# A fused mLSTM and two-layer MoE kernel: the state decay moves from a DRAM round trip and GpSimd to ScalarE and the broadcast in PSUM, and ScalarE's first queue is reordered

## The chip, the cores and the metric

The kernel runs on one core of a Trainium2 chip. A core has five engines with a queue each, which run in order and meet through semaphores: TensorE (PE; its weight loads are listed as PEld), VectorE (DVE), ScalarE (ACT), GpSimd (POOL) and SyncE (SP), which here issues all the DMAs. The metric is the device time of one execution in microseconds (us), as the median of several runs.

## The reference

Three stages follow each other; what counts is cut out here:

```
for t in range(S):                            # S = 768, batch 2, 8 heads, D = 40
    m_new  = max(f[t] + m, i[t])
    f_stab = exp(f[t] + m - m_new);  i_stab = exp(i[t] - m_new)
    C = f_stab * C + i_stab * outer(v[t], k[t])
    n = f_stab * n + i_stab * k[t]
    y[t] = sigmoid(o[t]) * (C @ q[t]) / max(|n . q[t]|, 1)
x = y as [1536, 320]
x = max(x @ w1, x @ w2, x @ w3) @ w_out       # 320 -> 768 -> 320
x = (h * tanh(softplus(h))) @ w_out2, h = x @ w_in   # 320 -> 2048 -> 320
```

## The kernel before

The recurrence is done in chunks of 128 steps. There are six chunks and two batches, so twelve units, numbered u = 2c + b for chunk c and batch b. For a unit, spread(u) makes PE broadcast the decay factors of all eight heads over the partitions (fp), decay(u) makes DVE scan them into the matrix of decays dt, scores(u) gives the products of keys and queries, decayed(u) multiplies the two, and numer(u) multiplies the result by the values. For chunks after the first, passed(u) makes PE broadcast the products of decays since the chunk's start (cp, 120 partitions: three heads of 40 rows), queries(u) multiplies the queries by them on DVE (cb), and numer(u) adds the part that comes from the state st of the batch. denom, gated, transpose_x and lower_x finish a unit: division, output gate, transposition, and the split of x into a rounded part xh and a rest xl, so that products in a rounded format keep precision. outer(u) gives the new part of the state (sp) and carry(u) adds it: state = state x decay of the whole chunk + masked new part.

The decay of a whole chunk comes from the running product cpr (16 partitions, one for each batch and head, 640 columns). Before the change its last column of each chunk goes to DRAM and is read back broadcast over all partitions (dsd, decs). The rest of cpr goes into the rows of fzr from 64 (rounded by ACT) and from 96 (the rest, by POOL), from which PE makes fp and cp of the later chunks.

Weights arrive as 64-bit words; each block is decoded by one ACT instruction (dec, L279) and three DVE instructions (low and dec, L286, L288, L290), and split into a rounded part (ACT, L301 to L303) and a rest (POOL, L304 to L306). Three buffers (raw) hold undecoded blocks.

The order of the first four units and of the first products is written out by hand in mlstm_moe_kernel (L384 to L541), engine by engine in program order. From PLAN0 on, the steps of the plans (a unit's first half a, its second half b, the products u, the weights w and o) are put into order by a scheduler in the framework; with issue_after, nothing of PLAN0 is put on an engine ahead of the instruction that is named (fence for PE, fdve for DVE, fpool for POOL, fsp for SP; ACT has none before the change). After PLAN1 come the second layer's weights and its products; that part isn't touched.

ACT has one table of functions loaded at a time; Exp and Sigmoid need different ones, and the load stands in ACT's queue as an instruction of its own.

Of the kernel before, what the change touches and what calls it, by code (L numbers as in the profile page):

```python
# [22 lines left out]
BH = B * H  # L23
VD = D + 1
# [13 lines left out]
NU = NC * B  # L38
# [4 lines left out]
def mlstm_moe_kernel(ctx, tc, fi0, fir, qk2, q3, nat, w13, wo1, wi2, wo2, ident, bmask, out):  # L43
    nc = tc.nc
# [2 lines left out]
    wpool = ctx.enter_context(tc.tile_pool(name="wpool", bufs=1))  # L47
    stage = ctx.enter_context(tc.tile_pool(name="stage", bufs=1))
    zpool = ctx.enter_context(tc.tile_pool(name="zpool", bufs=1))
    dram = ctx.enter_context(tc.tile_pool(name="dram", bufs=1, space=bass.MemoryType.DRAM))  # L50
    mmp = ctx.enter_context(tc.tile_pool(name="mmp", bufs=3, space=PSUM))

    zraw = zpool.tile([P, 3, NT], F32, tag="zraw", name="zraw")
# [6 lines left out]
    ac = at.enter_context(tc.tile_pool(name="ac", bufs=1))  # L60
    a2 = at.enter_context(tc.tile_pool(name="a2", bufs=2))
    pat = at.enter_context(tc.tile_pool(name="pat", bufs=1, space=PSUM))

    def bank(tag, name):
        if tag == "mm":
            return mmp.tile([P, 512], F32, tag=tag, name=name)
        return pat.tile([P, 512], F32, tag=tag, bufs=3 if tag == "sm" else 1, name=name)
# [4 lines left out]
    idt = ac.tile([P, P + 2 * BH + 1], F32, tag="idt", name="idt")  # L72
    idr = ac.tile([P, 4 * L], F32, tag="idr", name="idr")
    bmt = ac.tile([120, H], F32, tag="bmt", name="bmt")
    decs = ac.tile([P, BH, NC - 1], F32, tag="decs", name="decs")
    kps = [ac.tile([P, 9, D], F32, tag=f"kp{i}", name=f"kp{i}") for i in range(2)]
    vps = [ac.tile([P, 9, VD], F32, tag=f"vp{i}", name=f"vp{i}") for i in range(2)]
    qall = ac.tile([P, 2, 2, 4, L], F32, tag="qs", name="qall")
# [4 lines left out]
    fzr = ac.tile([P, (NC - 1) * L], F32R, tag="fzr", name="fzr")  # L83
# [21 lines left out]
    NR = NC - 1  # L105
# [6 lines left out]
    mtr = scr[0:BH, 3:5].rearrange("p k f -> p (k f)")[:, 0:LR + 1]  # L112
    cpr = scr[64:64 + BH, 4]
    z1r = scr[64:64 + BH, 5]
    dsd = dram.tile([BH, NR], F32, tag="dsd", name="dsd")

    unit = {u: {} for u in range(NU)}
    warm = zraw[:, 0, 0:256].bitcast(mybir.dt.bfloat16)
# [15 lines left out]
    def spread(u, tags=("sc0", "sc1")):  # L134
        c, b = u // B, u % B
        src = fzs if c == 0 else fzr[:, (c - 1) * L:c * L]
        fps = []
        for j in range(2):
            fp = bank(tags[j], f"fp{u}_{j}")
            for hh in range(4):  # L140
                r = b * H + 4 * j + hh
                nc.tensor.matmul(fp[:, hh * L:(hh + 1) * L], sel[:, r:r + 1].to_broadcast([P, P]), src, start=True, stop=True)  # L142
            fps.append(fp)
        unit[u]["fp"] = fps

    def passed(u, tag="sm"):
        c, b = u // B, u % B
        if c == 0:
            return
        ps = bank(tag, f"cp{u}")[0:120, 0:3 * L].rearrange("p (g t) -> p g t", g=3)  # L150
        for g in range(3):
            r = b * H + 3 * g
            nc.tensor.matmul(ps[:, g], sel40[:, r * D:(r + 3) * D], fzr[:, (c - 1) * L:c * L], start=True, stop=True)
        unit[u]["cp"] = ps

    def scores(u, banks=None):
        qk = qks[u % 2]
# [32 lines left out]
    def dummy(ps, n):  # L190
        for _ in range(n):
            nc.tensor.matmul(ps, warm[:, 0:P], warm, start=True, stop=True)  # L192
# [14 lines left out]

    def denom(u):
        num = unit[u]["it"]
        nq = a2.tile([P, H, 1], F32, tag="nq", name=f"nq{u}")  # L210
        den = a2.tile([P, H, 1], F32, tag="den", name=f"den{u}")
        nc.vector.tensor_scalar(nq, num[:, :, D:VD], -1.0, 1.0, op0=ALU.mult, op1=ALU.max)
        nc.vector.tensor_tensor(den, num[:, :, D:VD], nq, op=ALU.max)
        nc.vector.reciprocal(den, den)
        sg = unit[u]["sg"]
        nc.gpsimd.tensor_tensor(sg, sg, den.to_broadcast([P, H, D]), op=ALU.mult)
# [8 lines left out]
    def transpose_x(u, xp=None, fill=0):  # L225
        xh, xl = xs[u // 4]
        col = u % 4 * L
        xn = unit[u]["xn"]
        xp = bank("sm", f"xp{u}") if xp is None else xp
        dummy(xp, fill)  # L230
        xp = xp[:, 0:3 * L].rearrange("p (j t) -> p j t", j=3)
        for j in range(3):
            nc.tensor.transpose(xp[:, j], xn[:, j * P:(j + 1) * P], idt[:, 0:P])
        nc.scalar.activation(xh[:, :, col:col + L], xp, AF.Copy)  # L234
        unit[u]["xp"] = xp

    def lower_x(u):
        xh, xl = xs[u // 4]
# [17 lines left out]
    def carry(u):  # L256
        c, b = u // B, u % B
        sp = unit[u]["sp"]
        if c == 0:
            return nc.vector.tensor_tensor(st[b], sp[:, 0:H], bmt[:, 0:H].unsqueeze(2).to_broadcast([120, H, VD]), op=ALU.mult)  # L260
        nw = a2.tile([120, H, VD], F32, tag="nw", bufs=1, name=f"nw{u}")
        nc.vector.tensor_tensor(nw, sp[:, 0:H], bmt[:, 0:H].unsqueeze(2).to_broadcast([120, H, VD]), op=ALU.mult)
        nc.gpsimd.tensor_tensor(st[b], st[b], decs[0:120, b * H:(b + 1) * H, c - 1:c].to_broadcast([120, H, VD]), op=ALU.mult)
        nc.gpsimd.tensor_tensor(st[b], st[b], nw, op=ALU.add)

    raws = {}

# [116 lines left out]
    with tc.manual_schedule(engines={ET.PE, ET.DVE, ET.SP, ET.Activation, ET.Pool}):  # L384
# [46 lines left out]
        nc.scalar.activation(gT0, gp[:, 0:BH], AF.Copy)  # L431
        nc.vector.tensor_copy(zs[:, :, 0:1], fs[:, :, 0:1])
        nc.vector.memset(fs[:, :, 0:1], 0.0)
        scores(0)
        spread(1, ("sm", "sm"))
        scores(1, [bank("mm", "sc1_0"), bank("mm", "sc1_1")])
# [6 lines left out]
        gateo(0)  # L443
        decay(1)
        load_qk(2)
        nc.gpsimd.tensor_tensor(ir, ir, mr, op=ALU.subtract)
        values(1)
        keys(1)
        decayed(1, 0)
# [10 lines left out]
        denom(0)  # L460
        carry(0)
        nc.vector.tensor_tensor_scan(cpr, fr, z1r, 0.0, op0=ALU.mult, op1=ALU.add)
        nc.scalar.activation(ir, ir, AF.Exp)
        nc.sync.dma_start(dsd, cpr.rearrange("p (c t) -> p c t", c=NR)[:, :, L - 1])
        load_nat(3)
        nc.sync.dma_start(decs, dsd.rearrange("h c -> (h c)").partition_broadcast(P))
        fetch(w13[1], "w13_1")
        decay(2)
        gated(0)
        nc.scalar.activation(fzr[64:64 + BH], cpr, AF.Copy)  # L470
        it1 = bank("sm", "it1")
        dummy(it1, 3)
        numer(1, it1)
# [1 line left out]
        for c in range(NR):  # L475
            nc.tensor.transpose(gq[:, c * BH:(c + 1) * BH], ir[:, c * L:(c + 1) * L], idt[0:BH, 0:BH])
        scores(2, [bank("sm", "sc2_0"), bank("mm", "sc2_1")])
        nc.gpsimd.tensor_tensor(fzr[96:96 + BH], cpr, fzr[64:64 + BH].bitcast(F32), op=ALU.subtract)
        keys(2)
        nc.scalar.activation(gTr, gq[:, 0:NR * BH], AF.Copy)  # L480
        denom(1)
# [1 line left out]
        decayed(2, 0)  # L483
        decayed(2, 1)
        spread(3)
        xp0 = bank("mm", "xp0")
        dummy(xp0, 3)
        transpose_x(0, xp0)
        passed(2, "mm")
        values(2)  # L490
        scaled(w13[0], "w13_0")
        mg = merge("w13_0")
# [39 lines left out]
        fsp = fetch(w13[3], "w13_3")  # L532
        fence = outer(3, bank("sm", "sp3"))
        lower_x(2)
        transpose_x(3, bank("sm", "xp3"), 6)
        fetch(w13[2], "w13_2")
        fdve = lower_x(3)
        fpool = load_w13(1)
# [33 lines left out]
        for step in plan.split():  # L572
            act[step[0]](*[int(n) for n in step[1:].split(".")])

    with tc.issue_after(fence.ins), tc.issue_after(fdve.ins), tc.issue_after(fpool.ins), tc.issue_after(fsp.ins):
        follow(PLAN0)
    follow(PLAN1)
    at.close()
# [183 lines left out]
```

## Time and profile before

| | |
|---|---|
| median of 3 runs | 420.75 us (420.63 to 421.41) |
| profiled execution | 419.39 us |
| its span, first to last instruction | 417.6 us |
| PE busy | 401.2 us (96%) |
| DVE busy | 222.7 us (53%) |
| ACT busy | 164.7 us (39%) |
| POOL busy | 163.5 us (39%) |
| mean granted PE clock | 0.975 of full speed |

The busy times are those of one profiled execution. The share of the span is an average over stages of different kinds, so what an engine's work is worth is to be read stage by stage. The granted clock has two levels, 1.00 (2.4 GHz) and 0.50 (1.2 GHz); a value between is a mean over a stretch.

### The profile page before, as it was taken

How to read it: one execution, taken by the hardware profiler on the slowest of the kernel's cores; microseconds unless marked ns; L12 is line 12 of the kernel's file. 1: busy time of each engine (PE TensorE's matmuls, PEld its weight loads, DVE VectorE, ACT ScalarE, POOL GpSimd, SP SyncE). 2: the span in 40 equal slices, each digit the busy share in tenths (PEclk: the TensorE clock that was granted, in tenths of full speed). 3: DMA queues.
4: the chain of work that ended last, by engine and by line, in shares of the span. 5: the costliest groups of instructions: out<-in, count | busy, mean ns of one | idle time of the engine just before them, and what ended most of it. 6: DMA issues, size and time to landing. Idle time of an engine off the chain costs nothing.

```text
span 417.6 us, 6152 instructions
## 1 busy us (share of the span) xinstructions
PE 401.2 (96%) x2385; PEld 351.7 (84%) x2385; DVE 222.7 (53%) x334; ACT 164.7 (39%) x349; POOL 163.5 (39%) x163
## 2 busy tenths in 40 slices
PE   8979599997999999999999999999999999999996
PEld 4858488885879888888888888999988889999996
DVE  7957599989944644523852568993221112222221
ACT  3525354634222122127351657565332233434331
POOL 6645499798443322336772165654000000001000
PEclk9969798998999999999999999999999999999999
DMA  7669464571740300000430042500010000100000
GB/s 209 165 63 294 153 198 168 175 239 65 240 159 2 97 2 0 2 0 2 126 126 2 1 151 102 173 17 0 2 63 2 0 2 0 65 0 2 33 0 33
DMA packets 10650, 32.66 MB, mean 78 GB/s; under 512 B 1645, under 2 KB 4525, under 8 KB 10621
## 3 DMA queue, kind: packets, MB, share of 16 engines
q1 hardware_dynamic: 10621, 32.27, 25.4%
q8 instruction: 19, 0.31, 0.3%
q14 instruction: 10, 0.08, 0.1%
HBM read 30.30 MB, written 1.97 MB: 77 GB/s over the span
## 4 chain that ended last, share of the span: by engine, by line
PE 75%; DVE 11%; POOL 7%; issue 4%; DMA 2%; ACT 1%; POOLq 0%; DVEq 0%; ACTq 0%
PE h L333 21%; PE mm L333 16%; PE o L657 7%; PE o L655 7%; PE o L656 7%; PE it L205 2%; DVE dt L127 2%; DMA raw_w<-in_w_dram 2%; PE mz L365 2%; PE mz L363 2%; PE mz L364 2%; PE wps L192 1%; POOL w L304 1%; PE fp L142 1%; PE sc L161 1%
## 5 line engine op out<-in xcount | busy, mean ns | idle before, releaser
L639 DVE TENSOR_TENSOR gl<-g,gh 128x512 fp32r<-128x512 f32 (+1 forms) x64 | 38.3, 599 | 97.2 <-ACT g L638 97.2
L333 PE MATMUL mm<-xh,w 128*128 128x512 f32 x270 | 76.8, 413 | 3.5 <-ACT xh L234 3.1
L333 PE MATMUL h<-zh,wi 128*128 128x512 f32 (+1 forms) x320 | 66.9, 338 | 0.0
L333 PEld LDWEIGHTS mm<-xh,w 128*128 128x128 f32 x270 | 51.8, 198 | 15.1 <-ACT xh L234 3.2
L637 ACT ACTIVATE gh<-h 128x512 fp32r<-128x512 f32 (+1 forms) x64 | 31.4, 491 | 83.7 <-PE h L333 77.7
L657 PE MATMUL o<-wo,gl 128*128 128x320 f32 x192 | 59.4, 309 | 0.0
L656 PE MATMUL o<-wo,gh 128*128 128x320 f32 x192 | 59.4, 309 | 0.0
L655 PE MATMUL o<-wo,gh 128*128 128x320 f32 x192 | 59.2, 309 | 0.0
L333 PEld LDWEIGHTS h<-zh,wi 128*128 128x128 f32 x320 | 51.4, 189 | 4.8
L608 POOL TENSOR_TENSOR zl<-zraw,zh 128x512 fp32r<-128x512 f32 (+1 forms) x12 | 14.2, 1194 | 91.9 <-ACT zh L607 91.8
L333 PE MATMUL mm<-xl,w 128*128 128x512 f32 x162 | 48.2, 404 | 0.0
L333 PE MATMUL h<-zl,wi 128*128 128x512 f32 (+1 forms) x192 | 44.5, 338 | 0.0
L352 POOL TENSOR_TENSOR hl<-zraw,hh 128x512 fp32r<-128x512 f32 x18 | 25.6, 1422 | 44.2 <-ACT hh L351 44.1
L349 DVE TENSOR_TENSOR zraw<-zraw,mm 128x512 f32<-128x512 f32 x36 | 24.5, 681 | 31.0 <-PE mm L333 30.8
L655 PEld LDWEIGHTS o<-wo,gh 128*128 128x128 f32 x192 | 36.1, 188 | 1.3
L656 PEld LDWEIGHTS o<-wo,gh 128*128 128x128 f32 x192 | 36.1, 188 | 1.2
L333 PEld LDWEIGHTS mm<-xl,w 128*128 128x128 f32 x162 | 31.3, 196 | 6.7
L657 PEld LDWEIGHTS o<-wo,gl 128*128 128x128 f32 x192 | 36.1, 188 | 0.0
L333 PEld LDWEIGHTS h<-zl,wi 128*128 128x128 f32 x192 | 31.8, 188 | 4.1
L638 ACT ACTIVATE g<-h 128x512 f32<-128x512 f32 (+1 forms) x64 | 31.2, 487 | 0.0
L127 DVE TENSOR_TENSOR_SCAN dt<-fp,idr 128x512 f32<-128x512 f32 x24 | 28.3, 1208 | 2.4 <-PE fp L142 2.3
L205 PE MATMUL it<-vp,dt 128*128 128x41 f32 x192 | 25.2, 273 | 0.0
(137 smaller groups left out, 638.4 us busy)
## 6 DMA issues: line engine op xcount, KB each, us to landing
raw_wo<-in_wo_dram SPq DMA_DIRECT2D x11, 640.0 KB
na<-in_nat_dram SPq DMA_DIRECT2D x12, 484.0 KB
raw_w<-in_w_dram SPq DMA_DIRECT2D x9, 640.0 KB
raw_wi<-in_wi_dram SPq DMA_DIRECT2D x8, 640.0 KB
qall<-in_qk_dram SPq DMA_DIRECT2D x24, 160.0 KB
out_dram<-ob SPq DMA_DIRECT2D x12, 160.0 KB
q<-in_q_dram SPq DMA_DIRECT2D x10, 180.0 KB
idt<-in_ident_dram SPq DMA_DIRECT2D x1, 80.5 KB
```

The costliest lines, as they stand in the source:

```text
L127: nc.vector.tensor_tensor_scan(dtf[:, j * 512:(j + 1) * 512], unit[u]["fp"][j], idr, 0.0, op0=ALU.mult, op1=ALU.add)
L205: nc.tensor.matmul(it[:, h], t["dt"][:, h], vt[:, h], start=(c == 0), stop=(c == 0 or h == h1 - 1))
L333: nc.tensor.matmul(ps, a, r, start=(k == 0), stop=(k == 7))
L349: nc.vector.tensor_tensor(top, top, pss[i], op=ALU.max)
L352: nc.gpsimd.tensor_tensor(ls, top, h.bitcast(F32), op=ALU.subtract)
L608: nc.gpsimd.tensor_tensor(zl[:, j], zv[:, j], zh[:, j].bitcast(F32), op=ALU.subtract)
L637: mark[blk, m] = nc.scalar.activation(gh, ps, AF.Mish)
L638: nc.scalar.activation(g, ps, AF.Mish)
L639: low[blk, m] = nc.vector.tensor_tensor(gl, g, gh.bitcast(F32), op=ALU.subtract)
L655: nc.tensor.matmul(po, a, whi, start=(m == 0), stop=False)
L656: nc.tensor.matmul(po, a, wlo, start=False, stop=False)
L657: nc.tensor.matmul(po, l, whi, start=False, stop=(m == KF2 - 1))
```

## The change

The chunk's decay is no longer sent through DRAM. passed(u) copies the last column of cp of each of the three groups out of PSUM into a small tile dc (one ACT instruction). carry(u) scales the state with it in place, three ACT instructions (one for each group of heads, with a scale for each partition), and adds the masked new part with three DVE instructions in place of one; POOL's two instructions of carry and the tile nw go. In the first part that is ordered by hand: the exponential of the later chunks' input gates (ir) and the subtraction ahead of it are moved up, before ACT's first table change; the rounding of cpr into fzr and the subtraction behind it are moved up to where the write to DRAM stood; cp of unit 2 is put ahead of the first transposition, with one dummy product less; and PLAN0 is held back on ACT as well, behind xh of unit 3. denom saves a tile.

```
@@ passed
         unit[u]["cp"] = ps
+        if u < NU - B:
+            dc = a2.tile([120, 3, 1], F32, tag="dc", name=f"dc{u}")
+            nc.scalar.activation(dc, ps[:, :, L - 1:L], AF.Copy)
+            unit[u]["dc"] = dc
@@ denom
-        nq = a2.tile([P, H, 1], F32, tag="nq", name=f"nq{u}")
...
-        nc.vector.tensor_tensor(den, num[:, :, D:VD], nq, op=ALU.max)
+        nc.vector.tensor_scalar(den, num[:, :, D:VD], -1.0, 1.0, op0=ALU.mult, op1=ALU.max)
+        nc.vector.tensor_tensor(den, den, num[:, :, D:VD], op=ALU.max)
@@ carry
-        nw = a2.tile([120, H, VD], F32, tag="nw", bufs=1, name=f"nw{u}")
-        nc.vector.tensor_tensor(nw, sp[:, 0:H], bmt[:, 0:H].unsqueeze(2).to_broadcast([120, H, VD]), op=ALU.mult)
-        nc.gpsimd.tensor_tensor(st[b], st[b], decs[0:120, b * H:(b + 1) * H, c - 1:c].to_broadcast([120, H, VD]), op=ALU.mult)
-        nc.gpsimd.tensor_tensor(st[b], st[b], nw, op=ALU.add)
+        dc = unit[u]["dc"]
+        for g in range(3):
+            h1 = min(3 * g + 3, H)
+            nc.scalar.activation(st[b][:, 3 * g:h1], st[b][:, 3 * g:h1], AF.Copy, scale=dc[:, g])
+        for j in range(3):
+            nc.vector.scalar_tensor_tensor(st[b][:, j::3], sp[:, j:H:3], bmt[:, j:j + 1], st[b][:, j::3], op0=ALU.mult, op1=ALU.add)
@@ order of the first units
         nc.gpsimd.memset(fzr.bitcast(F32), 0.0)
+        nc.gpsimd.tensor_tensor(ir, ir, mr, op=ALU.subtract)
...
         nc.vector.memset(fs[:, :, 0:1], 0.0)
+        nc.scalar.activation(ir, ir, AF.Exp)
...
         load_qk(2)
-        nc.gpsimd.tensor_tensor(ir, ir, mr, op=ALU.subtract)
...
         nc.vector.tensor_tensor_scan(cpr, fr, z1r, 0.0, op0=ALU.mult, op1=ALU.add)
-        nc.scalar.activation(ir, ir, AF.Exp)
-        nc.sync.dma_start(dsd, cpr.rearrange("p (c t) -> p c t", c=NR)[:, :, L - 1])
+        nc.scalar.activation(fzr[64:64 + BH], cpr, AF.Copy)
+        nc.gpsimd.tensor_tensor(fzr[96:96 + BH], cpr, fzr[64:64 + BH].bitcast(F32), op=ALU.subtract)
         load_nat(3)
-        nc.sync.dma_start(decs, dsd.rearrange("h c -> (h c)").partition_broadcast(P))
         fetch(w13[1], "w13_1")
         decay(2)
         gated(0)
-        nc.scalar.activation(fzr[64:64 + BH], cpr, AF.Copy)
...
-        nc.gpsimd.tensor_tensor(fzr[96:96 + BH], cpr, fzr[64:64 + BH].bitcast(F32), op=ALU.subtract)
...
         spread(3)
+        passed(2, "mm")
         xp0 = bank("mm", "xp0")
-        dummy(xp0, 3)
+        dummy(xp0, 2)
         transpose_x(0, xp0)
-        passed(2, "mm")
...
-        transpose_x(3, bank("sm", "xp3"), 6)
+        fact = transpose_x(3, bank("sm", "xp3"), 6)
...
-    with tc.issue_after(fence.ins), tc.issue_after(fdve.ins), tc.issue_after(fpool.ins), tc.issue_after(fsp.ins):
+    with tc.issue_after(fence.ins), tc.issue_after(fdve.ins), tc.issue_after(fpool.ins), tc.issue_after(fsp.ins), tc.issue_after(fact.ins):
         follow(PLAN0)
```

The order on ACT in the first units, from the first gates to gTr, was this before (scr is the scratch tile that holds ir and cpr, sel the selection tile sel40, sg the gates of units 0 and 1, dl and xn those of the next units):

```order
L437 ACTIVATE fzr<-scr 16x640
L187 ACT_TABLE_LOAD
L187 ACTIVATE sg_229<-na_123 128x320
L131 ACTIVATE dl_234<-dt_231 128x8
L187 ACTIVATE sg_274<-na_130 128x320
L459 ACTIVATE sel_99<-idt 128x680
L463 ACT_TABLE_LOAD
L463 ACTIVATE scr<-scr 16x640
L131 ACTIVATE dl_297<-dt_294 128x8
L222 ACTIVATE xn_299<-xn_299 128x64
L470 ACTIVATE fzr<-scr 16x640
L480 ACTIVATE gTr<-gpr 128x80
```

After the change the same stretch of ACT's queue reads:

```order
L437 ACTIVATE scr<-scr 16x640
L441 ACTIVATE fzr<-scr 16x640
L188 ACT_TABLE_LOAD
L188 ACTIVATE sg_227<-na_119 128x320
L128 ACTIVATE dl_232<-dt_229 128x8
L188 ACTIVATE sg_271<-na_126 128x320
L462 ACTIVATE sel_96<-idt 128x680
L466 ACTIVATE fzr<-scr 16x640
L128 ACTIVATE dl_292<-dt_289 128x8
L222 ACTIVATE xn_294<-xn_294 128x64
L480 ACTIVATE gTr<-gpr 128x80
```

The exponential has gone ahead of the first table load, the second load is gone, and the second rounding into fzr stands ahead of dl and xn instead of behind them.

Further on in ACT's queue, around the last transposition of the first four units (sg_627 and sg_717 are the gates of units 4 and 5, xp_486 and xp_507 the transposed x of units 2 and 3), the order before is:

```order
L279 ACTIVATE dec_w_1_478<-raw_w_1_292 128x640
L187 ACTIVATE sg_627<-na_586 128x320
L234 ACTIVATE xh_107<-xp_486 128x3x128
L222 ACTIVATE xn_496<-xn_496 128x64
L187 ACTIVATE sg_717<-na_676 128x320
L279 ACTIVATE dec_w_2_571<-raw_w_2_518 128x640
L234 ACTIVATE xh_107<-xp_507 128x3x128
L301 ACTIVATE w_1_521<-dec_w_1_478 128x512
```

And after the change (st_98 and st_99 are the states of the two batches, now scaled here):

```order
L281 ACTIVATE dec_w_1_471<-raw_w_1_287 128x640
L235 ACTIVATE xh_103<-xp_479 128x3x128
L222 ACTIVATE xn_489<-xn_489 128x64
L235 ACTIVATE xh_103<-xp_500 128x3x128
L303 ACTIVATE w_1_514<-dec_w_1_471 128x512
L304 ACTIVATE w_1_514<-dec_w_1_471 64x128
L305 ACTIVATE w_1_514<-dec_w_1_471 64x128
L264 ACTIVATE st_98<-st_98,dc_352 120x123 x2
L264 ACTIVATE st_98<-st_98,dc_352 120x82
L264 ACTIVATE st_99<-st_99,dc_408 120x123 x2
L264 ACTIVATE st_99<-st_99,dc_408 120x82
L281 ACTIVATE dec_w_2_568<-raw_w_2_511 128x640
```

Both xh now stand ahead of the two gates and of dec_w_2, and six state scalings have come between w_1 and dec_w_2.

SP's queue, from the third unit's loads on (dsd is the tile in DRAM, na_287 the load of unit 3), is this before:

```order
L94 DMA qall<-in_qk_dram 40x1024 x2
L464 DMA dsd<-scr 80x1x1
L98 DMA na_287<-in_nat_dram 128x968
L102 DMA q_289<-in_q_dram 120x384
L466 DMA decs<-dsd 128x80
L271 DMA raw_w_1_292<-in_w_dram 128x1280
L271 DMA raw_w_3_500<-in_w_dram 128x1280
```

And after the change:

```order
L92 DMA qall<-in_qk_dram 40x1024 x2
L96 DMA na_283<-in_nat_dram 128x968
L100 DMA q_285<-in_q_dram 120x384
L273 DMA raw_w_1_287<-in_w_dram 128x1280
L273 DMA raw_w_3_493<-in_w_dram 128x1280
```

The write to DRAM and the read back are gone from between the loads; the rest keeps its order.

## Rows read from the trace of the kernel before

**Rows 1.** Stretches: length; busy us of PE, PEld, DVE, ACT, POOL; clock, DMA share, GB/s.

```profile
20.50:23.90 3.40, 0.07 (x3) 0.04 (x1) 2.60 (x8) 1.44 (x4) 1.55 (x2) 0.76 1.16 41
23.90:29.50 5.60, 5.60 (x31) 4.74 (x33) 1.18 (x2) 1.28 (x2) 2.08 (x3) 0.53 0.68 72
29.50:43.10 13.60, 13.60 (x106) 11.08 (x102) 10.52 (x20) 5.81 (x13) 7.62 (x8) 1.00 0.89 264
43.10:48.10 5.00, 0.35 (x3) 0.15 (x2) 0.59 (x2) 2.68 (x7) 0.64 (x2) 0.81 0.62 243
48.10:53.00 4.90, 4.90 (x12) 3.83 (x13) 4.90 (x7) 1.94 (x6) 4.07 (x6) 0.50 0.00 2
53.00:117.00 64.00, 60.37 (x342) 49.94 (x340) 61.02 (x85) 26.68 (x56) 51.65 (x50) 0.95 0.56 186
117.00:409.00 292.00, 292.00 (x1720) 262.76 (x1721) 123.97 (x186) 114.82 (x246) 82.93 (x75) 1.00 0.12 38
```

**Rows 2.** Chain that ended last: start us, us, engine, tile and line.

```profile
16.54 1.81 DVE scr L462
...
21.41 0.74 ACT fzr L470
...
38.25 8.55 DMA raw_w<-in_w_dram
```

**Rows 3.** Instructions in order of time, POOL, PE, DVE, 20 to 34 us.

```profile
22.27 1.53 POOL L478 TENSOR_TENSOR fzr<-scr,fzr 16x640 fp32r<-16x640 f32 x1 [5.28 <-ACT fzr L470]
...
23.86 1.97 PE L142 MATMUL fp<-fzr,sel 128*128 128x128 f32 x8 [3.33 <-POOL fzr L478]
...
28.32 0.56 DVE L177 TENSOR_TENSOR cb<-cp,q 120x384 f32<-120x384 f32 x1 [5.15 <-PE cp L153]
...
33.51 0.56 DVE L177 TENSOR_TENSOR cb<-cp,q 120x384 f32<-120x384 f32 x1 [1.36 <-PE cp L153]
```

**Rows 4.** SP's queue of DMA issues in order of time, 18 to 28 us.

```profile
18.37 0.68 SPq L464 DMA_DIRECT2D dsd<-scr  x1
...
26.60 0.35 SPq L466 DMA_DIRECT2D decs<-dsd  x1
27.01 0.89 SPq L271 DMA_DIRECT2D raw_w<-in_w_dram  x2
```

**Rows 5.** Instructions in order of time, ACT and PE, 39 to 49 us.

```profile
39.48 0.80 ACT L279 ACTIVATE dec_w<-raw_w 128x640 f32<-128x640 f32 x1
...
42.60 0.51 PE L153 MATMUL cp<-fzr,sel 128*120 128x128 f32 x3
...
43.66 0.47 ACT L187 ACTIVATE sg<-na 128x320 f32<-128x320 f32 x1 [3.37 <-DMA na<-in_nat_dram]
...
47.56 0.48 ACT L234 ACTIVATE xh<-xp 128x384 fp32r<-128x384 f32 x1
...
48.09 2.50 PE L333 MATMUL mm<-xh,w 128*128 128x512 f32 x5 [3.06 <-ACT xh L234]
```

**Rows 6.** Groups by line, 48 to 117 us: count, busy us, mean ns; one line's extremes; waits.

```profile
L263 POOL TENSOR_TENSOR st<-st,decs 120x328 f32<-120x328 f32 x5 | 4.9, 975 | 0.2
L264 POOL TENSOR_TENSOR st<-st,nw 120x328 f32<-120x328 f32 x4 | 4.7, 1178 | 0.1
L262 DVE TENSOR_TENSOR nw<-sp,bmt 120x328 f32<-120x328 f32 x4 | 1.9, 486 | 0.0
L213 DVE TENSOR_TENSOR den<-it,nq 128x8 f32<-128x8 f32 x3 | 0.5, 159 | 0.0
L288 DVE SCALAR_TENSOR_TENSOR low_w<-dec_w,low_w 128x640 int32<-128x640 int32 x7 | 7.8, 1120 | 0.2
L288 DVE SCALAR_TENSOR_TENSOR low_w<-dec_w,low_w x7: 792/899/1708, 52.9 to 82.2; 128x640 int32<-128x640 int32 x7
L302 ACT ACTIVATE w<-dec_w 64x128 fp32r<-64x128 f32 x8 | 2.4, 295 | 0.0
...
POOL st L263 <- PE it L203: 11.1, 2, 6.5
```

More of the change, by code (lines that the diff above doesn't have):

```diff
@@ L49, in mlstm_moe_kernel @@
     zpool = ctx.enter_context(tc.tile_pool(name="zpool", bufs=1))
-    dram = ctx.enter_context(tc.tile_pool(name="dram", bufs=1, space=bass.MemoryType.DRAM))
     mmp = ctx.enter_context(tc.tile_pool(name="mmp", bufs=3, space=PSUM))
@@ L74, in mlstm_moe_kernel @@
     bmt = ac.tile([120, H], F32, tag="bmt", name="bmt")
-    decs = ac.tile([P, BH, NC - 1], F32, tag="decs", name="decs")
     kps = [ac.tile([P, 9, D], F32, tag=f"kp{i}", name=f"kp{i}") for i in range(2)]
@@ L114, in mlstm_moe_kernel @@
     z1r = scr[64:64 + BH, 5]
-    dsd = dram.tile([BH, NR], F32, tag="dsd", name="dsd")
     unit = {u: {} for u in range(NU)}
@@ L209, in denom @@
         num = unit[u]["it"]
-        nq = a2.tile([P, H, 1], F32, tag="nq", name=f"nq{u}")
         den = a2.tile([P, H, 1], F32, tag="den", name=f"den{u}")
-        nc.vector.tensor_scalar(nq, num[:, :, D:VD], -1.0, 1.0, op0=ALU.mult, op1=ALU.max)
-        nc.vector.tensor_tensor(den, num[:, :, D:VD], nq, op=ALU.max)
+        nc.vector.tensor_scalar(den, num[:, :, D:VD], -1.0, 1.0, op0=ALU.mult, op1=ALU.max)
+        nc.vector.tensor_tensor(den, den, num[:, :, D:VD], op=ALU.max)
         nc.vector.reciprocal(den, den)
@@ L233, in transpose_x @@
             nc.tensor.transpose(xp[:, j], xn[:, j * P:(j + 1) * P], idt[:, 0:P])
-        nc.scalar.activation(xh[:, :, col:col + L], xp, AF.Copy)
         unit[u]["xp"] = xp
+        return nc.scalar.activation(xh[:, :, col:col + L], xp, AF.Copy)
     def lower_x(u):
```

## The prediction

> **What bounds the kernel now.** I read the stretches of the span first [rows 1]. From 117 us to 409 us TensorE (PE) is busy all 292.00 us at a granted clock of 1.00: there the kernel is bound by PE, and nothing of the change lies in it except work of engines that wait for PE. What can move is when that stage starts. Before it lie two others. From 53 to 117 us VectorE (DVE) is busy 61.02 of 64 us and GpSimd (POOL) 51.65: DVE is the bound there, and it waits for almost nothing. Until 53 us no engine is full, and the losses can be counted: PE does 0.07 us of work from 20.5 to 23.9 us, and 0.35 us from 43.1 to 48.1 us; after each of these holes the clock stands at about half, 1.2 GHz (0.53 until 29.5 us, 0.50 until 53 us).
>
> Then the chain of waits [rows 2] and the order of time around the two holes say what each waits for. The first hole: the product of decays (DVE, scr, L462) is ready at 16.54 + 1.81 = 18.35 us, but ScalarE (ACT) rounds it only at 21.41, POOL subtracts from 22.27 (it had waited 5.28 us), and PE, free since 23.86 - 3.33 = 20.53, starts fp of unit 3 at 23.86. DVE is done with decayed(2) at 28.32 - 5.15 = 23.17 and waits the 5.15 us for cp of unit 2 [rows 3]. The second hole: ACT stands from 40.28 to 43.66 us for na of unit 4, then for raw_w_2 (landed at 38.25 + 8.55 = 46.80 us), and so reaches xh of unit 3, the last input of the first big product, at 47.56; PE starts at 48.09 [rows 2, 5].
>
> SyncE's queue (SP) shows where the late transfers come from. The write of dsd is issued from 18.37 to 19.05, and decs, which waits for it, leaves at 26.60; both fetches of w13 behind decs leave at 27.01 [rows 4]. Meanwhile the DMA engines are marked busy (share 1.16 and 0.68) while moving 41 and 72 GB/s, against 264 GB/s afterwards [rows 1].
>
> **The change, part by part.** The profiled execution took 419.39 us, of which the span is 417.6; the median of three runs is 420.75, 1.36 us above it. The sum is made against 419.39.
>
> *Passed decay and the exponential (first hole).* The exponential of ir and its table load go away from between sel40 and the rounding of cpr, and the rounding now stands ahead of dl and xn of unit 2. It can start at 18.4; POOL, idle there, follows from 19.1 to 20.6 (1.53 us as in its row), so fp of unit 3 starts at about 20.7, right behind scores. PE's hole shrinks from 3.33 to some 0.2 us, and the clock has no reason to fall. cp(2), now ahead of xp, is ready at about 22.2, before DVE is free at 23.17. So DVE's whole wait goes: 5.15 us, and queries(2) starts at 23.2 instead of 28.32. Of the moved pieces, the earlier exponential delays the rounding into fzr of the first sixteen rows by about 0.74 us (the row of the same shape, L470 in [rows 2]), but POOL takes that up only behind vp of unit 0, so it costs some 0.1 us; the earlier subtraction of mr fills a gap of POOL; one dummy product less is 0.2 us on a PE that is no longer late. The next late thing is cp(3), for which DVE waits 1.36 us before as well as after. The second removed table load stood ahead of a gate that nobody waits for: I cost it at nothing. Term A: -5.2 us, with 3.3 (PE's hole alone) and 6.5 (DVE's next wait gone too) as ends.
>
> *ACT's queue before the first big product (second hole).* The gates of units 4 and 5 and dec_w_2 now stand behind xh of unit 3, and so do the new state scalings. What is late next is PE's own order: cp of unit 4 ends at 42.60 + 0.51 = 43.11, the last transpose and xh take 0.3 and 0.5 us more, so the first big product could have started at 43.9 instead of 48.09. Term B: -4.2 us. It needs raw_w_2 in time: its buffer comes free when DVE has decoded w_0, 5.2 us earlier than now, so it is issued at about 33 instead of 38.25, and DVE wants it at about 39.2. Before, it took 8.55 us among six other transfers; now both w13 fetches leave before 20 us, behind na of unit 3, since nothing in SP's queue waits there any more. I take 6 us and no loss; with 8.55 the loss is 2.4 us. So B lies between -1.8 and -4.2. The half clock from 48.1 to 53 us should go as well, but PE is not the bound behind it: no gain booked.
>
> *State update (from 53 us on, eight units).* POOL loses two instructions in each; in 48 to 117 us these are 4.9 + 4.7 = 9.6 us [rows 6]. DVE gives up nw (0.486 us) and gets three smaller ones: with 0.159 us for the eight-column instruction as the fixed part, 3 x 0.159 + (0.486 - 0.159) = 0.80, so +0.32 us for each of four units, +1.3 us on the bound. ACT gets three scalings and a copy; the nearest row has 0.295 us [rows 6], so 32 x 0.295 = 9.4 us over the kernel, some half of it in this stage, where ACT is busy 26.68 of 64 us: hidden, unless its order makes it wait. What DVE gains from a quieter POOL no row shows directly. The seven low_w instructions of L288 average 1.120 us where the fastest takes 0.792: 0.33 us of stretch each; with L286 and L290 there are some 36 such instructions, 12 us in all, and 9.6 of the 51.65 us that POOL is busy is 19%, so 2.3 us. Net of 1.3: term C is -1.0 us, between +1.3 (no relief) and -8.3 (all 9.6 us come back to DVE).
>
> The Trainium skill, "SBUF — State Buffer", section "SBUF: two separate sides", says that VectorE and GpSimd share one pair of ports as a lock held for a whole instruction, the loser waiting in full; the stretched L288 rows, up to 1.708 us, fit that. By it every POOL instruction removed could free DVE for its length, the lower end of C; it is the second rival.
>
> Sum: -5.2 - 4.2 - 1.0 = -10.4, so 409.0 us on the profiled execution's scale and 410.4 us as a median of runs. The stage from 117 us on is PE alone and shifts as a whole.
>
> **Rivals.** First, the transfers stay late. The slow stretch from 20.5 to 29.5 us would then not be the small write's doing, but that of the loads around it. For it: 80 elements of 4 bytes are little for 7.5 us of waiting. Against it: the rate is back as soon as decs is gone. SP would get free but the data not, DVE would wait for raw_w_2 in place of ACT, and B falls away: 414.6 us.
>
> The Trainium skill, "DMA: Bandwidth & Descriptors", section "Anatomy of one DMA", gives about 2 us as the fixed cost of a transfer on GpSimd's path, most of it the receipt of the write; this kernel's row on SP's path has 26.60 - 19.05 = 7.5 us. By the page's figure decs would have left near 21, and 5.6 us of the block would belong to something that remains, which is this rival; the row decides for the write.
>
> Second, POOL's relief comes back to DVE in full: C is -8.3, 403.1 us. PE would just allow it: from 48 to 117 us it loses about 2.5 us to the clock at first, then 3.6 us idle and some 3 us of low clock (0.95 of 64 us).
>
> Third, slower: ACT's queue becomes the bound from 53 to 117 us. A scaling must wait for PE's read of the state and for dc; POOL, which did this before, waited 11.1 us for it in two places [rows 6]. ACT serves its queue in order, and behind the scaling stand splits of weights and evictions of mm, for which PE and DVE wait. Price: 9.4 + 11.1 = 20.5 us, 430.9 us if all of it is exposed; it makes the kernel slower once more than 10.4 us are. Against it: two waits in eight units are few, and ACT is busy only 42% of that stage.
>
> Fourth, no change: DVE's stage keeps its end because its order, which the scheduler made anew, holds it up for what the start gained. Nothing in its rows of before shows such a wait.
>
> **How the numbers follow.** Forecast 0.60, first rival 0.15, second 0.15, third 0.06, fourth 0.04. The forecast's own range is 406.5 to 414 (upwards most of the ends of A and B, downwards A's and half of C's). The whole range, 403 to 416, holds the first three cases, with C's upper end on top of the first rival. About 0.2%, 0.8 us, is what a measurement here tells from no change; the forecast and the first two rivals are all faster by more: 0.90, same 0.04, slower 0.06.
>
> **What would show it.** The fp matmuls of unit 3 at about 20.7 us and a clock of 1.00 from 20 to 45 us; cb of unit 2 at 23.2; both w13 fetches issued before 20 us; the first big product at 38.7 us (right for A and B; at 43 for A alone); ACT's state scalings with little idle time in front; DVE's L288 nearer to 0.8 us; and the last wait of PE near 107 instead of 117 us. PE idle for ACT's evictions or splits from 45 us on would prove the forecast wrong.

## The result and the profile after

The changed kernel takes 408.72 us (median of 4 runs, 408.44 to 409.31); the kernel before took 420.70 beside it (4 runs, 420.63 to 421.41). The ratio is 0.9713, 95% interval 0.9696 to 0.9730. A second measurement gave 408.80 us and 0.9732 (0.9708 to 0.9757). The profiled execution took 409.31 us, with a span of 407.5, against 419.39 and 417.6 before: 10.1 us less. The medians differ by 12.0, since the profiled execution of before was quicker than the four timed beside it (420.63 to 421.41) and that of after was the slowest of its four.

The stretches of the kernel after, with the columns of [rows 1]:

```profile
20.50:23.90 3.40, 3.28 (x32) 2.92 (x32) 3.33 (x9) 1.81 (x6) 2.86 (x5) 1.00 1.01 341
23.90:29.50 5.60, 5.60 (x43) 4.31 (x42) 4.13 (x9) 1.87 (x8) 1.72 (x2) 1.00 0.80 268
29.50:38.00 8.50, 8.05 (x63) 6.77 (x61) 6.92 (x13) 3.89 (x12) 5.48 (x6) 1.00 0.55 169
40.00:53.00 13.00, 13.00 (x73) 10.70 (x72) 12.90 (x21) 8.06 (x22) 8.90 (x12) 1.00 0.55 175
53.00:95.00 42.00, 37.12 (x201) 30.33 (x201) 40.64 (x61) 21.84 (x49) 32.05 (x33) 0.90 0.51 177
95.00:117.00 22.00, 22.00 (x129) 18.88 (x127) 12.41 (x23) 6.23 (x15) 5.04 (x5) 0.96 0.48 157
117.00:400.00 283.00, 283.00 (x1675) 255.22 (x1675) 121.88 (x186) 115.49 (x250) 74.62 (x65) 1.00 0.11 36
```

Both holes of TensorE are gone, and the clock stays at 1.00 from 20 to 53 us. In the first window PE works 3.28 us instead of 0.07, and the DMA engines, busy as before, move 341 GB/s instead of 41. The stage of PE alone starts earlier, and from 95 us on DVE is no longer full (12.41 of 22 us).

The instructions that answer to [rows 3 to 5], in order of time (SPq is SyncE's queue; brackets hold the idle time before and what ended it):

```profile
16.62 1.09 SPq L273 DMA_DIRECT2D raw_w<-in_w_dram  x2
...
19.04 1.53 POOL L467 TENSOR_TENSOR fzr<-scr,fzr 16x640 fp32r<-16x640 f32 x1 [2.31 <-ACT fzr L466]
...
20.62 1.11 PE L139 MATMUL fp<-fzr,sel 128*128 128x128 f32 x8 [0.29 <-POOL fzr L467]
...
22.81 0.55 DVE L178 TENSOR_TENSOR cb<-cp,q 120x384 f32<-120x384 f32 x1
...
28.03 0.56 DVE L178 TENSOR_TENSOR cb<-cp,q 120x384 f32<-120x384 f32 x1 [1.40 <-ACT dc L154]
...
37.59 0.49 ACT L235 ACTIVATE xh<-xp 128x384 fp32r<-128x384 f32 x1 [1.17 <-PE xp L233]
...
38.13 1.43 PE L335 MATMUL mm<-xh,w 128*128 128x512 f32 x5 [0.58 <-ACT xh L235]
...
40.83 0.76 ACT L281 ACTIVATE dec_w<-raw_w 128x640 f32<-128x640 f32 x1
```

The first cb comes 5.51 us earlier than in [rows 3], the first big product 9.96 us earlier than in [rows 5]. From there the chain of waits runs through DVE until 64.6 us, mostly through splits on POOL until 76.3, through DVE again until 85.3, and then through PE to the end:

```profile
84.07 1.22 DVE dt L124
85.33 1.16 PE sc L162 x8
86.49 2.43 PE mm L335 x5
```

So the last wait of PE in this execution is at 85 us and not near 107. Low clock follows it (0.61 from 85.3 to 90 us, 0.50 until 95). At xp of unit 7 the lead is still 10 us, and the end of the span comes 10.1 us earlier.

### The profile page after: what moved, and what is told of

It is laid out like the page before. It is cut to its first block, busy times and chain, and to the rows that moved or that the text cites. A ratio compares the mean times of both kernels' runs of the same rounds, so it can differ in the third digit from the quotient of the medians.

```text
span 407.5 us, 6181 instructions
## 1 busy us (share of the span) xinstructions
PE 397.1 (97%) x2384; PEld 348.7 (86%) x2384; DVE 222.0 (54%) x350; ACT 170.4 (42%) x379; POOL 146.7 (36%) x147
## 4 chain that ended last, share of the span: by engine, by line
PE 86%; DVE 7%; issue 3%; POOL 2%; ACT 1%; DVEq 0%; POOLq 0%
PE h L335 22%; PE mm L335 20%; PE o L657 7%; PE o L655 7%; PE o L656 7%; PE it L206 4%; PE sc L162 3%; PE mz L365 2%; PE mz L366 2%; PE mz L367 2%; PE fp L139 2%; DVE dt L124 2%; PE it L204 2%; PE wps L193 1%; PE sp L252 1%
## 5 line engine op out<-in xcount | busy, mean ns | idle before, releaser
L335 PE MATMUL mm<-xh,w 128*128 128x512 f32 x270 | 75.8, 407 | 0.6 <-ACT xh L235 0.6
L335 PEld LDWEIGHTS mm<-xh,w 128*128 128x128 f32 x270 | 50.9, 194 | 11.4 <-ACT xh L235 0.8
```

The source lines that it names most:

```text
L335: nc.tensor.matmul(ps, a, r, start=(k == 0), stop=(k == 7))
```

## The experiments

All times are medians beside runs of the kernel before (419.8 to 420.6 us in these rounds). "First product" is the start of the first big product in the profiled execution, 48.09 us before and 38.13 after (38.60 when profiled again).

**The changed kernel again.**

> The changed kernel once more, as the measure for the kernels of this round: 408 to 409.5 us, first product of w13 at 38.1.

408.80 us (6 runs, 408.16 to 409.57), first product at 38.60.

### One part undone

**No ACT fence.**

```
-    ..., tc.issue_after(fsp.ins), tc.issue_after(fact.ins):
+    ..., tc.issue_after(fsp.ins):
```

> The changed kernel, but the planned part no longer has to wait for xh(3) on ACT, so sg4, sg5 and the decode of w13_2 stand again ahead of xh(3) in ACT's queue; no DRAM trip, early rounding and the new state update stay. Theory (ACT's queue order makes the second hole): sg4 sits at about 34 us and waits for its load na(4); first product of w13 at 41 to 43 us instead of 38.1, a PE hole with half clock behind it, 411 to 414 us. Rival (the second hole was only the late transfers behind the DRAM write, now gone): sg4 and dec_w_2 find their data there, ACT loses only their own run time, about 1 us, first product by 39.2, 408.5 to 410 us.

411.38 us (4 runs, 410.55 to 412.48; ratio 0.9798, 0.9771 to 0.9825), first product at 39.58. ACT and PE in order of time:

```profile
38.37 0.78 ACT L281 ACTIVATE dec_w<-raw_w 128x640 f32<-128x640 f32 x1 [1.57 <-POOL w L308]
39.58 1.43 PE L335 MATMUL mm<-xh,w 128*128 128x512 f32 x5 [2.01 <-ACT xh L235]
```

The time is the theory's (411 to 414); the mechanism is neither's. na(4) is there, so sg4 doesn't wait (the rival was right in that). But the decode of w13_2 waits 1.57 us for a buffer that POOL is still splitting, and xh(3) stands behind it. What the fence keeps out of ACT's queue is a wait for POOL, once no DMA is late. Counted from fp(3), the first product comes 18.94 us behind it instead of 17.51, so 1.4 of the 2.6 us are lost there. The rest comes later, and no trace shows where.

**Late rounding.**

```
-        nc.scalar.activation(fzr[64:64 + BH], cpr, AF.Copy)   # behind the scan
-        nc.gpsimd.tensor_tensor(fzr[96:96 + BH], cpr, ...)
...
         gated(0)
+        nc.scalar.activation(fzr[64:64 + BH], cpr, AF.Copy)
...
         scores(2, ...)
+        nc.gpsimd.tensor_tensor(fzr[96:96 + BH], cpr, ...)
```

> The changed kernel with the two roundings of the passed decay (ACT copy into fzr, POOL subtraction) back at their old places: ACT's behind gated(0), POOL's behind the scores of unit 2. No DRAM trip, early exponential, the rest as changed. Theory (the place in the queues makes the first hole): fzr on POOL ends 1 to 3 us later than 20.6, PE idle about that long ahead of fp(3), 410 to 413 us, with a larger loss if the clock falls to half again. Rival (the hole came from the late transfers behind the DRAM write and from the exponential with its table load, not from the place of the rounding): fzr comes less than 0.8 us later, 408.5 to 409.5 us.

413.64 us (4 runs, 411.99 to 413.68; 0.9841, 0.9813 to 0.9868), first product at 42.40. The windows show the clock (0.70 after the hole, 1.00 in the kernel after):

```profile
20.50:23.90 3.40, 0.43 (x4) 0.43 (x4) 2.21 (x7) 1.36 (x4) 1.93 (x2) 1.00 0.94 347
23.90:29.50 5.60, 5.60 (x39) 4.22 (x37) 3.88 (x5) 2.55 (x7) 3.40 (x6) 0.70 0.35 112
```

and the order of time why PE had nothing:

```profile
21.89 1.53 POOL L478 TENSOR_TENSOR fzr<-scr,fzr 16x640 fp32r<-16x640 f32 x1 [5.27 <-ACT fzr L470]
...
23.47 1.11 PE L139 MATMUL fp<-fzr,sel 128*128 128x128 f32 x8 [3.25 <-POOL fzr L478]
```

The loads are quick here (347 GB/s), and the hole is back: it is the place of the rounding in the queues of ACT and POOL. The loss of 4.8 us is the theory's larger case, in which the clock falls as well.

**The trip kept for nothing.**

```
+        nc.sync.dma_start(dsd, cpr.rearrange(...)[:, :, L - 1])
         load_nat(3)
+        nc.sync.dma_start(decs, dsd.rearrange(...).partition_broadcast(P))
         fetch(w13[1], "w13_1")
```

> The changed kernel with the DRAM trip put back for nothing: SyncE writes the 80 decays to DRAM ahead of load_nat(3) and reads them back into a tile that nobody reads; nothing else on any engine changes. Theory (the trip costs as a block on SyncE's queue: na(3), w13_1 and w13_3 are issued 7 to 10 us later; the rounding and ACT's order cover part of it): the fetches of w13_1 and w13_3 issue at about 26 to 27 us instead of 16.6, raw_w lands at about 38, first product at 41 to 48 us, 412 to 418 us. Rival (the trip was hidden anyway and the reordering alone gave the gain): first product still by 39, 408.4 to 409.5 us.

417.03 us (6 runs, 414.89 to 418.21; 0.9929, 0.9902 to 0.9956), first product at 43.87. No engine but SyncE has a new instruction, and 8.2 of 12 us are lost, as the theory said (412 to 418). SyncE's queue:

```profile
18.24 0.68 SPq L471 DMA_DIRECT2D dsd<-scr  x1
19.02 0.52 SPq L98 DMA_DIRECT2D na<-in_nat_dram  x1
19.59 0.41 SPq L102 DMA_DIRECT2D q<-in_q_dram  x1
26.43 0.35 SPq L473 DMA_DIRECT2D decs<-dsd  x1
26.84 0.89 SPq L276 DMA_DIRECT2D raw_w<-in_w_dram  x2
```

The write again takes 26.43 - 18.92 = 7.5 us until decs may leave. The window of 20.5 to 23.9 us reads:

```profile
20.50:23.90 3.40, 3.13 (x31) 2.77 (x32) 3.33 (x10) 1.67 (x6) 2.31 (x4) 1.00 1.15 40
```

That is 40 GB/s where it was 341. The window lies before the read leaves, so the low rate comes with the write alone, and it isn't for want of loads: na of unit 3, issued at 19.02, keeps ACT waiting until 30.87. The trip shows up twice: as a block on SyncE's queue, and in the loads that cross with it. How the 8.2 us divide between the two, no run separates.

**The exponential late.** It and its POOL subtraction go back to their old places; the rounding stays early.

```
-        nc.scalar.activation(ir, ir, AF.Exp)    # ahead of scores(0)
...
         nc.vector.tensor_tensor_scan(cpr, fr, z1r, 0.0, ...)
+        nc.scalar.activation(ir, ir, AF.Exp)
         nc.scalar.activation(fzr[64:64 + BH], cpr, AF.Copy)
```

> The changed kernel with the exponential of the rest's input gates (and the POOL subtraction ahead of it) back at its old place, right ahead of the rounding on ACT, where it brings a table load of 1.3 us and, with the run of the exponential, 2 us or more between the scan and the rounding; the rounding itself stays early. Theory: fp(3) at 22 to 23.5 instead of 20.6, 410 to 412 us. Rival (ACT has slack there: the scan is what the rounding waits for): fp(3) by 21, 408.3 to 409.3 us.

408.37 us (6 runs, 408.05 to 410.10; 0.9726, 0.9700 to 0.9752), no difference from 408.80, though fp(3) starts at 21.69 and the first product at 39.20, each 0.6 us later than in the changed kernel profiled again (21.09 and 38.60). Other traces with the same start put fp(3) at 20.62 to 21.37, so little of that need be the exponential. ACT in order of time:

```profile
16.12 1.28 ACT L465 ACT_TABLE_LOAD   x1
17.42 0.74 ACT L465 ACTIVATE scr<-scr 16x640 f32<-16x640 f32 x1
19.23 0.73 ACT L466 ACTIVATE fzr<-scr 16x640 fp32r<-16x640 f32 x1 [1.08 <-DVE scr L464]
```

Table load and exponential end at 18.16, and the rounding still waits 1.08 us for the scan. The rival holds for the time: this part of the change is worth nothing.

**The state update back on POOL, twice.** First with three smaller multiplications by ACT's dc, then in the very form of before (dc copied to nine columns, one multiplication):

```
-            nc.scalar.activation(st[b][:, 3 * g:h1], st[b][:, 3 * g:h1], AF.Copy, scale=dc[:, g])
...
-            nc.vector.scalar_tensor_tensor(st[b][:, j::3], sp[:, j:H:3], bmt[:, j:j + 1], ...)
+        nc.vector.tensor_tensor(nw, sp[:, 0:H], bmt..., op=ALU.mult)
+        nc.gpsimd.tensor_tensor(st[b], st[b], dc[:, 0:H].to_broadcast([120, H, VD]), op=ALU.mult)
+        nc.gpsimd.tensor_tensor(st[b], st[b], nw, op=ALU.add)
```

> The changed kernel, but the state is decayed and summed by POOL as before (VectorE multiplies the PSUM product by the mask, POOL multiplies the state by the same decay column and adds), without the DRAM trip; the orders of the first 38 us stay as changed. Theory (the state update is worth next to nothing, since from 85 us on TensorE has work waiting whatever POOL does): first product at 38.1, 408.5 to 410 us. Rival (POOL relieved of some 10 us is worth much, through ports or through the splits that TensorE waits for): 412 to 416 us. A third outcome, that the two or three small operations of VectorE per unit cost more than they give: 406 to 408 us.

> The changed kernel with the state update on POOL in the very form of the kernel before: one multiplication of the 328 columns and one addition (about 2.1 us per unit, where the earlier trial with three smaller multiplications took 3.3), the decay taken from ACT's copy of the broadcast, without the DRAM trip; VectorE multiplies by the mask once. Theory (it is POOL's busy time that counts: the earlier trial lost 2.1 us with 13.2 us on POOL, and 9.6 us lose less): 408.8 to 410.2 us. Rival (the loss is VectorE's stretch by POOL's updates, or their place in POOL's queue, not their length): 410.3 to 411.5 us, VectorE's second decode step again at 1.1 us instead of 0.90.

410.87 us (5 runs, 410.76 to 411.40; 0.9787, 0.9762 to 0.9812) and 410.06 us (6 runs, 409.43 to 410.31; 0.9742, 0.9710 to 0.9773). First product at 38.66 and 38.35, so all of the loss comes later. The first trial's expectation, next to nothing, missed, and so did its rival (412 to 416). Groups of the second, 38 to 107 us (count, busy us, mean ns), POOL and DVE:

```profile
L264 POOL TENSOR_TENSOR st<-st,dc 120x328 f32<-120x328 f32 x5 | 5.4, 1088 | 0.1
L265 POOL TENSOR_TENSOR st<-st,nw 120x328 f32<-120x328 f32 x4 | 3.8, 952 | 0.2
...
L289 DVE SCALAR_TENSOR_TENSOR low_w<-dec_w,low_w 128x640 int32<-128x640 int32 x7 | 8.3, 1190 | 0.2
```

With 9.2 us on POOL the loss is 1.3 us (410.06 - 408.72 to 408.80), with 13.2 it was 2.1. The theory of the second trial gives the time, and the rival's sign is there too: DVE's second decode step takes 1.190 us instead of 0.903. By the ratios the second trial loses only 0.4 us (against 0.9732) to 1.2 us (against 0.9713), and its interval overlaps those of the kernel after, so that this part gains at all rests on both trials together.

### One part alone, on the kernel before

**First hole alone.** Rounding and exponential early, passed decay of unit 2 ahead of the transpose, by the lines of the diff above; trip, ACT's queue and POOL's update as before.

> The kernel before with the first hole's part of the change alone: rounding of the passed decay right behind the scan, the exponential and its POOL subtraction early, passed decay of unit 2 ahead of the transpose. The DRAM trip, ACT's queue and the state update on POOL stay. The prediction's step, term A by itself: first hole gone, first product at 43, about 415 us. Rival (while the trip delays the loads, the 5 us saved ahead of the second hole are waited for again in it: na(4) and w13_2 land no earlier): fp(3) at 20.6 all the same, but first product at 45.5 to 48, 417.5 to 420.5 us.

420.57 us (12 runs, 419.46 to 422.83; 1.0018, 0.9993 to 1.0043): nothing gained, which is the rival's case, with a first product even later than it said (49.49 against 45.5 to 48). In order of time:

```profile
21.22 1.11 PE L142 MATMUL fp<-fzr,sel 128*128 128x128 f32 x8 [0.29 <-POOL fzr L465]
...
31.48 0.56 DVE L177 TENSOR_TENSOR cb<-cp,q 120x384 f32<-120x384 f32 x1 [4.26 <-DMA q<-in_q_dram]
...
43.95 0.47 ACT L187 ACTIVATE sg<-na 128x320 f32<-128x320 f32 x1 [5.20 <-DMA na<-in_nat_dram]
...
49.49 2.50 PE L333 MATMUL mm<-xh,w 128*128 128x512 f32 x5 [4.17 <-ACT xh L234]
```

The first hole closes, and its 5 us are waited for again: 4.26 at the second cb, which stands until 31.48 for a q that was issued behind the write, and 5.20 instead of 3.37 at na(4).

**ACT fence alone.**

```
+            fact = transpose_x(3, bank("sm", "xp3"), 6)
...
+    ..., tc.issue_after(fact.ins):
```

> The kernel before with one thing of the change alone: the planned part waits for xh(3) on ACT as well, so sg4, sg5 and the decode of w13_2 stand behind it. The DRAM trip, the late rounding and the state update on POOL stay. With the trip kept, na(4) lands late, and sg4 waits 3.37 us for it ahead of xh(3). Theory (the queue order and the late transfers make the second hole together, so either cure takes most of it): first product 3 to 4.5 us earlier than 48.09, 416 to 418 us. Rival (w13_0 and w13_1, or the keys of unit 3, are late as well, so the place in ACT's queue decides nothing while the trip stays): first product after 46.5, 419.5 to 421 us.

417.93 us (12 runs, 416.64 to 420.28; 0.9939, 0.9919 to 0.9959), first product at 44.50. With the trip kept the fence gives 3.6 us there and 2.5 us in the time: the theory.

**Trip gone, state on ACT, the rest as before.**

> Of the change only the DRAM trip is gone and the state update is on ACT; the rounding, the exponential, the passed decay of unit 2 and ACT's queue stand as in the kernel before. Theory (the three cures act on different waits and add up: late rounding cost 4.8 us, the missing ACT fence 2.6): fp(3) at 23.5 to 25, first product of w13 near 43.4, 414.5 to 417.5 us. Rival (with the rounding late, xh(3) comes after na(4) has landed, and the fence is worth nothing more): first product at 42 to 42.8, 413 to 414.4 us.

416.10 us (6 runs, 414.36 to 416.93; 0.9892, 0.9854 to 0.9930), first product at 46.68. The time is the theory's; the first product is 3 us later than it said, though fp(3) at 24.82 lies in its 23.5 to 25. The trace has more behind fp(3) than the theory added up: DVE waits 5.37 us ahead of the first cb and 1.82 ahead of the second, and the decode of w13_2 waits 1.58 us for POOL ahead of xh(3), as without the fence. Windows:

```profile
20.50:23.90 3.40, 0.99 (x16) 0.79 (x16) 3.33 (x9) 1.44 (x4) 0.66 (x1) 1.00 1.03 309
23.90:29.50 5.60, 4.68 (x19) 3.81 (x21) 0.23 (x2) 0.68 (x3) 3.66 (x5) 0.53 0.49 187
```

The loads are quick without the write whatever the order is (309 GB/s), and the first hole stays, with its half clock.

### Two attempts at more

**Filling PE's wait at 85 us.**

```
+        for _ in range(fill):      # 16 for unit 6
+            nc.tensor.matmul(ps[:, 0:L], sel[:, 0:1].to_broadcast([P, P]), fzr[:, 0:L], ...)
```

> The changed kernel with 16 small products of no use (128 columns, 0.14 us each by the broadcasts of the decay, 2.2 us in all) written to the bank of unit 6's passed decay ahead of it, where TensorE waits 2.02 us for VectorE at 85.3 and then runs at half clock until about 97; the planner moves some products around it. Theory (what ended the gain of the state update is this wait and the half clock behind it: 12 us at about 0.55 of the clock): the clock stays 1.00, TensorE saves up to 5 us, but VectorE is busy without a break until 95, so part is given back in waits: 404 to 407.5 us. Rival (TensorE is so far behind or VectorE so full that the clock costs nothing): 408 to 409.5 us.

408.97 us (6 runs, 408.79 to 410.21): no gain, and inconclusive. PE in order of time:

```profile
83.56 1.98 PE L149 MATMUL cp<-fzr,sel 128*128 128x128 f32 x16
85.37 0.48 PE L153 MATMUL cp<-fzr,sel 128*120 128x128 f32 x3
86.08 0.49 PE L165 MATMUL sc<-qall 64*128 64x128 f32 x2 [0.23 <-DVE dt L124]
89.30 2.07 PE L165 MATMUL sc<-qall 64*128 64x128 f32 x14 [2.73 <-DVE dt L124]
```

The filler ran as meant, but the planner then set both halves of the scores in one row, and PE waits 2.73 us for the second bank instead. No run separates what a kept clock is worth there, but the late exponential's trace bears on it. It has the same wait, and its clock holds:

```profile
86.43 1.16 PE L162 MATMUL sc<-qall 64*128 64x128 f32 x8 [2.02 <-DVE dt L124]
...
106.21 0.91 PE L233 MATMUL xp<-idt,xn 128*128 128x128 f32 x3 [0.21 <-DVE xn L221]
```

```profile
85.30:90.00 4.70, 2.87 (x16) 2.18 (x17) 4.67 (x5) 2.49 (x6) 2.48 (x3) 1.00 0.18 50
```

There the clock stays at 1.00 until 105 us, and PE waits for DVE again, 1.9 us in all behind that wait. The first product was 1.07 us later than in the kernel after and the end of the span 0.8 us later (408.3 against 407.5), so the kept clock gave 0.3 us at most, less than two executions differ by. That speaks for the rival: what the clock gives, DVE takes back.

**x's low part off DVE.**

```
+        if 4 <= u < 8:
+            nc.scalar.activation(xr, unit[u]["xp"], AF.Copy)
+            return nc.gpsimd.tensor_tensor(xl[...], xr, xh[...], op=ALU.subtract)
```

> The changed kernel with the low part of x of units 4 to 7 taken off VectorE: ACT copies the transposed block out of PSUM and POOL subtracts, as for units 0 and 1. VectorE loses 4 x 0.55 = 2.2 us in the stage where it is busy without a break, ACT gains 4 copies (about 1.6 us), POOL 4 subtractions (about 4 us). Theory (VectorE is the bound of that stage until TensorE takes over): 406.5 to 408 us. Rival (POOL's added time and ACT's order hold up the weight splits and stretch VectorE's decodes, as the state update on POOL did): 409 to 411 us.

411.08 us (5 runs, 410.77 to 411.69; 0.9789, 0.9755 to 0.9822): slower than the changed kernel, and as the rival said (409 to 411). Its way isn't shown: the second decode step is not stretched (0.902 us); PE waits 1.9 us for xn and 3.8 for dt. No version here is faster than the changed kernel by more than the spread of its own runs.

## Why the prediction was right, and where its steps were not

**The sum.** -10.4 us were forecast on the profiled execution's scale, -10.1 came. The median of 408.72 lies 1.7 us under the 410.4 because 1.36 us were added for a profiled execution quicker than its median, while that of after turned out 0.6 us slower than its own. Agreement to 0.3 us is in part luck: the two traces of the changed kernel already differ by 0.8 us in span (407.5 and 406.7), and by the medians the gain is 11.7 to 12.0 us.

**Term A, the first hole: -5.2 forecast, -5.5 at cb of unit 2.** fp(3) at 20.62 (20.7 forecast), cb at 22.81 (23.2), and the 1.4 us ahead of the next cb stayed, as said. Two points of its working fall. The exponential and its table load were counted in; late, they cost nothing. And A does not stand by itself: the prediction had the first product "at 43 for A alone", and alone, with the trip kept, it came at 49.49, with no gain in time. In the changed kernel the rounding is worth 4.8 us, and the waits for q and na(4) above say why: only when loads are prompt does work that comes earlier find its data. The place of cp of unit 2, the dummy product less and denom's tile were not undone by themselves.

**Term B, the second hole: -4.2 forecast, 9.96 - 5.51 = 4.45 measured.** The first product at 38.13 (38.7 forecast), both fetches at 16.62, raw_w_2 issued at 32.20 (33 forecast), and DVE's first decode step of it runs at 38.59 without a wait: the assumed 6 us were about right. But B is two things that the prediction booked together under ACT's order. With the write gone and the fence left out, the first product is only 1.4 us late. So some 3 of the 4.45 us come from the removed write: without it na(4) and raw_w_2 are there when ACT asks for them. In the whole time the fence is worth 2.6 us where the rest is changed and 2.5 where it alone is.

**How the parts add.** Alone: rounding (with the exponential and the place of cp) 0, fence 2.5, trip with the state update 3.7 us (419.83 - 416.10). Undone one at a time: rounding 4.8, fence 2.6, trip 8.2, state 1.3 to 2.1. The parts alone add up to 6, the parts undone to about 17, for 12 in all. The fence is worth the same either way; the rounding and the trip pay in full only when the other is mended too.

**Term C, the state update: -1.0 forecast, -1.3 to -2.1 by undoing it (medians).** Its two halves, 38 to 107 us of the kernel after (count, busy us, mean ns):

```profile
L290 DVE SCALAR_TENSOR_TENSOR low_w<-dec_w,low_w 128x640 int32<-128x640 int32 x7 | 6.3, 903 | 0.1
L288 DVE TENSOR_SCALAR low_w<-raw_w 128x640 int32<-128x640 int32 x7 | 5.7, 816 | 0.0
...
L266 DVE SCALAR_TENSOR_TENSOR st<-sp,bmt,st 120x123 f32<-120x123 f32 (+1 forms) x12 | 3.1, 319 | 0.0
...
L264 ACT ACTIVATE st<-st,dc 120x123 f32<-120x123 f32 x10 | 3.6, 389 | 1.7 <-PE it L204 1.7
L264 ACT ACTIVATE st<-st,dc 120x82 f32<-120x82 f32 x5 | 1.8, 351 | 0.5 <-PE it L204 0.5
```

DVE pays 3.1 us for four units instead of 1.9 [rows 6], the 1.2 us extra that was worked out as 1.3. The second decode step fell from 1.120 us [rows 6] to 0.903, and the second POOL trial has 1.190: seven times 0.29 is 2 us of relief. All decode steps of DVE up to 130 us together take 43.3 us before, 40.5 and 41.3 in the two traces after, and 43.1 and 43.0 in the POOL trials, so the 2.3 us forecast were about right.

That this relief is the whole of C is not shown. The prediction took DVE for the only bound of that stage, but in the kernel before the chain of waits runs through POOL for much of it, state updates included (start us, us, engine, tile and line):

```profile
60.50 0.89 POOL st L264
...
88.24 1.44 POOL st L264
```

From 48 to 117 us the chain's pieces on POOL add up to 25.7 us before, 7.5 after, and 41.4 and 31.3 in the two trials. So the update on POOL can cost time by its own length, as well as by stretching DVE's steps, and no run separates the two. The traces of before and after by themselves show nothing of C, since the lead is 9.96 us at 38 us and 10.1 at the end; its size rests on the medians of the trials.

One price was too low: an ACT scaling of 123 columns takes 0.389 us and one of 82 columns 0.351, not 0.295. The Trainium skill, "ScalarE: Activation LUTs", section "What ACT_TABLE_LOAD costs", gives 186 ns and 0.833 ns per element for an ACTIVATE, and some 93 ns more for each operand that is a pointer: by that an estimate of 0.381 us for the 123 columns scaled by dc, and the trace's 0.389 us agrees. The row that the prediction used has no such operand.

**The last wait of PE: forecast near 107 us, found at 85.** The prediction let DVE's stage end where it ended before, less the lead. But PE, with products waiting from 38 us and half clock after 85, became the bound sooner. This hangs on the execution: where the clock stayed at 1.00 after that wait, as with the late exponential, the last wait is at 106.21, as forecast.

**The rivals.** Late transfers (414.6): with the write gone 291 to 357 GB/s flow in the window where it was 41, whatever else is changed, and 40 to 50 as soon as it is back. The 7.5 us come and go with the write. POOL's relief in full (403.1): undone, the update costs 2 us and not 8. ACT's queue as bound (430.9): the scalings wait 1.7 + 0.5 = 2.2 us for PE in the view above, and from 45 us on PE waits for no split and no eviction of ACT. No change: refuted by the end of the span.

```profile
PE sc L162 <- DVE dt L124: 3.5, 3, 2.0
PE fp L139 <- DVE dt L167: 1.3, 1, 1.3
```

These are all of PE's waits from 53 to 117 us after (us, times, longest): for DVE alone.

**Two bounds.** The ranges don't follow from the prediction's own terms. Downwards, A's end and half of C's give 410.4 - 1.3 - 3.65 = 405.4 us and not 406.5; C's upper end on top of the first rival gives 414.6 + 2.3 = 416.9 us and not 416. The result lies within either.

## What to carry to other kernels

A tiny transfer to DRAM on the queue that also feeds the loads is priced by what stands behind it and crosses with it, not by its bytes. Where several late things follow one another, price each both ways, alone and undone from the whole; the difference tells which one must be mended before the others pay. And before moving work between engines, see which one waits last in that stage: what a full engine gains ends where the next one is full.

## What the runs showed of the hardware

- A write of 80 elements of 4 bytes from SBUF to DRAM holds the next transfer that depends on it for 6.82 to 7.55 us in the four kernels that have it, and while it is under way the DMA engines read as busy (share 1.15 to 1.49 in the window of 20.5 to 23.9 us) at 40 to 50 GB/s, against 291 to 357 GB/s at a share of about 1.0 in the kernels without it. Loads issued right behind it land late: with the first hole alone, q of unit 3, issued at 20.04, holds up DVE until 31.48 us. Why they are held up no run separates.
- Where PE waited 2.02 us until 85.33 us, the granted clock was 0.61 in the next 4.7 us and 0.50 until 95 us. The same wait of 2.02 us, until 86.43 us with the late exponential, left it at 1.00. With 0.29 and 0.58 us of waiting at 20 and 38 us it stayed at 1.00.
- From 38 to 107 us DVE's second decode step takes 1.08 to 1.19 us in the five kernels with POOL's state update and 0.89 to 0.97 without it, though the step itself is the same.
